# A state-space layer and two feed-forward layers on one core: the first feed-forward layer in four blocks of one piece and four of two, instead of six and three

## The chip, the cores and the metric

The kernel runs on one core of a Trainium2 chip. The metric is the device time of one execution in microseconds, smaller is better. A measurement is the median of several executions.

## What is computed

A chunked state-space scan (4 sequences, 8 heads, 768 tokens, head size 32, state size 16) gives 3072 tokens of 256 numbers. Two feed-forward layers follow, each 256 to 2048 to 256, the first with a leaky ReLU, the second with a squared ReLU:

```python
for c in range(nc):                       # chunks of 32 tokens
    cum = np.cumsum(la, axis=-1)
    M = einsum('bhin,bhjn->bhij', Cc, Bc) * L          # L: causal decay
    y[:, :, sl] = einsum('bhij,bhjd->bhid', M, xc) \
                + einsum('bhin,bhnd->bhid', Cc, state) * exp(cum)
    state = decay_full * state + sum_j(Bc x xc * decay_from_j)
x = y as (tokens, 256)
h = x @ moe_w_in;  x = maximum(0.01 * h, h) @ moe_w_out
h = maximum(x @ moe2_w_in, 0);  x = (h * h) @ moe2_w_out
```

The matrix products of the feed-forward layers are made of three TensorE products of rounded parts (high, low), so that the result keeps float32 accuracy.

## The kernel before

The tokens are cut into 12 pieces of 256 tokens (p0 to p11). The scan works piece by piece: `scan_a` and `scan_b` are generators that give way after every few instructions, and `stage(k)` runs `scan_b(k - 1)` and `scan_a(k)` side by side. What a piece gives are the tiles `yh` and `yl` (lines 448 and 449), 256 tokens wide.

One piece needs on TensorE the products S (lines 389 and 390, stationary `kbd`), Y1 (lines 418 to 420, stationary `xbh` and `xbl`) and Y2 (lines 439 and 440, stationary `sbd`). These four stationary tiles are block-diagonal, have one buffer each, and are filled by `diag` (line 353), four small DMAs on SP's queue for each tile, so 16 for a piece. SP issues in order. Ahead of the pieces p6 to p8 stand scales of their whole sequence, for which tiles `all` are loaded and squared (line 274).

The first feed-forward layer takes the pieces in blocks, `BLOCKS`: six blocks of one piece (256 columns) and three of two (512 columns). A block is one `One` object. Its hidden rows are worked in steps, 96 over all blocks: a step of a one-piece block does two groups of 128 hidden rows with 256 columns each, a step of a two-piece block one group with 512 columns. In every step `hmm` does the first product (`in_products`, lines 470 to 472), `act` evicts it (two on ScalarE, lines 507 and 508, one on VectorE, line 509), and `omm` does the second product (lines 532, 533, 538) two steps later in a block of one piece and three steps later in a block of two (`LAG`). `finish` copies the block's result (line 547). The block of p0 is in float32 (lines 493, 526). Steps are counted from 0 here: 0 to 7 are p0's block, 32 to 39 p4's, 40 to 47 p5's, and step 48 begins the block of p6 and p7.

How far the scan is emitted at a step says `due`: every block has a place (twice its first step less its `LEAD`) by which the stages for its pieces are to be emitted, with a ramp of `RATE` towards it. Weights of the second layer are prepared in between, from block `W2_FROM` on (`w_one`: lines 132, 135, 143, 152, 174, 175). This sets the order of the source. Behind it the framework's own scheduler makes each engine's final order, so that it differs from the source's by several steps.

Of the kernel before, what the change touches and what calls it, by code (L numbers as in the profile page):

```python
# [32 lines left out]
KK = 2.0**-12  # L33
E23 = float(1 << 23)

BLOCKS = [1, 1, 1, 1, 1, 1, 2, 2, 2]
NG = NP // 2
LAG = {1: 2, 2: 3}
LAG2 = 2
W_AHEAD = 4  # L40
RATE = 1.4 / KO
LEAD = [0, 4, 12, 12, 10, 8, 6, 4, 4]
W2_FROM = 3
NSTEP = 15
APART = 3
PRE = 8
# [9 lines left out]
def ssd_moe_kernel(ctx: ExitStack, tc: tile.TileContext, in1, in2, w1i, w1o, w2i, w2o, out):  # L56
# [395 lines left out]
    blocks, q0 = [], 0  # L452
    for n in BLOCKS:
        blocks.append((q0, n))
# [216 lines left out]
    for i, (p0, n) in enumerate(blocks):  # L671
        todo += [(i, list(range(m, m + 2 // n))) for m in range(0, KO, 2 // n)]
    at_ = [2 * [i for i, _ in todo].index(i) for i in range(len(blocks))]
    starts = [
        (at - lead, p0 + n + (0.5 if p0 + n <= APART else 1)) for at, lead, (p0, n) in list(zip(at_, LEAD, blocks))[1:]
    ]

    def due(at):
        return max(nb - max(RATE * (b - at), 0) for b, nb in starts)

    pend = []

# [18 lines left out]
    for i, ms in todo:  # L701
        p0, n = blocks[i]
# [6 lines left out]
        pos += 2  # L709
        ph_.act(ms)  # L710
        stages_to(due(pos + 2))
        pend.append((ph_, ms, ms[-1] == KO - 1))
        if len(pend) > LAG[n]:
# [8 lines left out]
        else:  # L722
            first_w = w_full and w_full[0][0][0] == "1"
            acc += 1.5 if first_w else 0 if i < W2_FROM else (0.4 if i < len(blocks) - 1 else 1.5)
            while acc >= 1:
# [75 lines left out]
```

## Time and profile before

| | |
|---|---|
| median of 3 runs | 606.81 us (606.45 to 608.25) |
| the profiled execution | 606.45 us, its span 604.7 us |
| TensorE busy in the span | 572.1 us (95%) |
| VectorE, ScalarE busy | 455.6 us (75%), 445.5 us (74%) |
| mean granted TensorE clock | 0.998 |

The profile prints for each engine its busy time and share of the span, and the span again in 40 slices with a digit for the busy tenths of each. A matmul is recorded longer than the distance to the next, since matmuls overlap; how fast TensorE goes is read from the starts. The timeline prints start, length, engine, line, operation and tiles, and in brackets an idle time ahead with what ended it.

### The profile page before, as it was taken

To read this page: it belongs to the slowest core of one execution; us is meant where nothing else is said; L and a number is where in the kernel's file an instruction comes from. 1 tells how busy PE (TensorE), PEld (TensorE's weight loads), DVE (VectorE), ACT (ScalarE), POOL (GpSimd) and SP (SyncE) were. 2 spreads that over 40 slices of the span, in tenths; PEclk is the share of its full clock that TensorE was granted. 3 is DMA by queue.
4 is the path that set the end of the run, shared out by engine and by line. 5 is a ranking of instruction groups with operands and counts; after the bars stand their busy time and mean duration, and the time that the engine had idled before them with its cause. 6 is when DMAs were issued, how large, how long until landed. Compare 5 with 4: busy or idle time off the path is not lost.

```text
span 604.7 us, 11654 instructions
## 1 busy us (share of the span) xinstructions
PE 572.1 (95%) x4610; PEld 516.3 (85%) x4610; DVE 455.6 (75%) x774; ACT 445.5 (74%) x715; POOL 5.2 (1%) x15
## 2 busy tenths in 40 slices
PE   0399999999999999999999999999999999999996
PEld 0388899999999878888888889989999999999996
DVE  6999989569984979567655468787777877877765
ACT  6999876479676868556665588877878777777773
POOL 3000000000000000000000000000000000000000
PEclk9999999999999999999999999999999999999999
DMA  8864845573576663131210000010000100100101
GB/s 295 289 160 129 234 111 116 129 193 92 113 187 189 163 166 36 36 62 46 69 36 0 1 2 0 2 36 1 9 28 1 35 1 2 36 1 0 36 1 35
DMA packets 113574, 46.50 MB, mean 77 GB/s; under 512 B 94448, under 2 KB 103280, under 8 KB 113520
## 3 DMA queue, kind: packets, MB, share of 16 engines
q1 hardware_dynamic: 113520, 45.76, 28.3%
q8 instruction: 36, 0.59, 0.4%
q14 instruction: 18, 0.15, 0.1%
HBM read 36.83 MB, written 3.15 MB: 66 GB/s over the span
## 4 chain that ended last, share of the span: by engine, by line
PE 86%; DVE 7%; ACT 4%; issue 2%; DMA 1%; DVEq 0%; ACTq 0%
PE hp L470 13%; PE hp L471 13%; PE hp L472 13%; PE o L532 4%; PE o L611 4%; PE o L538 4%; PE o L533 4%; PE o L609 4%; PE o L610 4%; PE oo L533 3%; PE oo L538 3%; PE oo L532 3%; PE Ym L611 3%; PE Ym L610 3%; PE Ym L609 3%
## 5 line engine op out<-in xcount | busy, mean ns | idle before, releaser
L509 DVE TENSOR_TENSOR g<-t,g 128x512 fp32r<-128x512 f32 x88 | 60.5, 687 | 52.6 <-ACT t L508 52.4
L587 DVE TENSOR_TENSOR tl<-ts,th 128x1024 fp32r<-128x1024 f32 x48 | 58.8, 1226 | 47.1 <-ACT th L585 47.1
L507 ACT ACTIVATE g<-hp 128x512 fp32r<-128x512 f32 x88 | 52.3, 594 | 47.2 <-PE o L538 33.7
L470 PE MATMUL hp<-yl,w1i 128*128 128x256 f32 (+1 forms) x256 | 83.4, 326 | 0.7 <-DVE yl L449 0.7
L471 PE MATMUL hp<-yh,w1i 128*128 128x256 f32 (+1 forms) x256 | 83.2, 325 | 0.0
L472 PE MATMUL hp<-yh,w1i 128*128 128x256 f32 (+1 forms) x256 | 83.0, 324 | 0.0
L575 ACT ACTIVATE b<-hp 128x512 f32<-128x512 f32 x96 | 57.2, 596 | 33.0 <-PE hp L472 32.8
L470 PE MATMUL hp<-xl,w2i 128*128 128x512 f32 x192 | 75.4, 393 | 0.0
L471 PE MATMUL hp<-xh,w2i 128*128 128x512 f32 x192 | 75.3, 392 | 0.0
L472 PE MATMUL hp<-xh,w2i 128*128 128x512 f32 x192 | 74.8, 389 | 0.0
L585 ACT CAST th<-ts 128x1024 fp32r<-128x1024 f32 x48 | 50.3, 1047 | 16.8 <-DVE ts L584 16.8
L470 PEld LDWEIGHTS hp<-yl,w1i 128*128 128x128 f32 x256 | 48.7, 190 | 4.9 <-DVE yl L449 1.1
L508 ACT ACTIVATE t<-hp 128x512 f32<-128x512 f32 x88 | 52.2, 593 | 0.0
L472 PEld LDWEIGHTS hp<-yh,w1i 128*128 128x128 f32 x256 | 48.7, 190 | 3.7
L471 PEld LDWEIGHTS hp<-yh,w1i 128*128 128x128 f32 x256 | 48.7, 190 | 3.7
L576 ACT ACTIVATE b<-b 128x1024 f32<-128x1024 f32 x48 | 50.9, 1061 | 1.1
L586 DVE TENSOR_TENSOR bl<-b,bh 128x768 fp32r<-128x768 f32 x48 | 45.7, 952 | 0.0
L582 DVE TENSOR_TENSOR ts<-b 128x512 f32<-128x512 f32 x48 | 33.2, 691 | 14.5 <-ACT b L576 13.5
L472 PEld LDWEIGHTS hp<-xh,w2i 128*128 128x128 f32 x192 | 36.1, 188 | 7.8
L470 PEld LDWEIGHTS hp<-xl,w2i 128*128 128x128 f32 x192 | 36.2, 189 | 6.3
L471 PEld LDWEIGHTS hp<-xh,w2i 128*128 128x128 f32 x192 | 36.2, 189 | 5.8
L581 ACT CAST bh<-b 128x768 fp32r<-128x768 f32 x48 | 40.1, 835 | 1.3
(167 smaller groups left out, 1571.4 us busy)
## 6 DMA issues: line engine op xcount, KB each, us to landing
in<-in SPq DMA_DIRECT2D x12, 640.0 KB, 4.9
in<-in SPq DMA_DIRECT2D x12, 512.0 KB, 5.7
all<-in SPq DMA_DIRECT2D x15, 384.0 KB, 4.3
wst<-w1i SPq DMA_DIRECT2D x8, 512.0 KB, 6.6
wst<-w1o SPq DMA_DIRECT2D x8, 512.0 KB, 6.4
wst<-w2i SPq DMA_DIRECT2D x8, 512.0 KB, 7.4
wst<-w2o SPq DMA_DIRECT2D x8, 512.0 KB, 4.2
out_t<-r SPq DMA_DIRECT2D x24, 128.0 KB, 1.7
```

The lines of the kernel that those rows point to most:

```text
L470: nc.tensor.matmul(hp, wh[:, k, c], xl[:, :, k], start=(k == 0), stop=False)
L471: nc.tensor.matmul(hp, wh[:, k, c], xh[:, :, k], start=False, stop=False)
L472: nc.tensor.matmul(hp, wl[:, k, c], xh[:, :, k], start=False, stop=(k == KI - 1))
L507: nc.scalar.activation(g[:, 0], hp, AF.Lrelu)
L508: nc.scalar.activation(t, hp, AF.Lrelu)
L509: nc.vector.tensor_tensor(g[:, 1], t, g[:, 0].bitcast(F32), ALU.subtract)
L532: nc.tensor.matmul(self.o[d], wl[:, c], gh, start=(m == 0 and (d == 0 or self.n == 2)), stop=False, **kw)
L575: nc.scalar.activation(b[:, 2 * i : 2 * i + 2], hp.rearrange("p (n t) -> p n t", n=2), AF.Relu)
L576: nc.scalar.activation(b, b, AF.Square)
L585: nc.scalar.copy(th, t)
L586: nc.vector.tensor_tensor(bl, b[:, 1:], bh.bitcast(F32), ALU.subtract)
L587: nc.vector.tensor_tensor(tl, t, th.bitcast(F32), ALU.subtract)
```

## The change

The pieces p4 and p5 form one block of two pieces. The table `LEAD` has new numbers from the fifth entry on, the scan's ramp towards the new block is 1.3 times as steep, and second-layer weights start in the same block as the two-piece work. The number of steps stays 96.

```diff
-BLOCKS = [1, 1, 1, 1, 1, 1, 2, 2, 2]
+BLOCKS = [1, 1, 1, 1, 2, 2, 2, 2]
-LEAD = [0, 4, 12, 12, 10, 8, 6, 4, 4]
-W2_FROM = 3
+LEAD = [0, 4, 12, 12, 11, 12, 8, 6]
+W2_FROM = 4
...
     starts = [
-        (at - lead, p0 + n + (0.5 if p0 + n <= APART else 1)) for at, lead, (p0, n) in list(zip(at_, LEAD, blocks))[1:]
+        (at - lead, p0 + n + (0.5 if p0 + n <= APART else 1), RATE * (1.3 if i == 4 else 1))
+        for i, (at, lead, (p0, n)) in enumerate(zip(at_, LEAD, blocks))
+        if i > 0
     ]
...
-        return max(nb - max(RATE * (b - at), 0) for b, nb in starts)
+        return max(nb - max(r * (b - at), 0) for b, nb, r in starts)
```

The engines' orders are the same in both kernels up to step 31 of the first layer (TensorE), up to the scale factors of p6's sequence (VectorE, ScalarE), and on SP up to the loads for p7. Then they part. On SP, before; `kbd`, `xbh` and `xbl` are here those of p6, `sbd<-t_2262` is that of p5, and the `kbd` behind it that of p7:

```order
L123 DMA wst<-w2i 128x2x256 x2
L353 DMA kbd<-kmx 32x16x32 x4
L353 DMA xbh<-xh 32x16x32 x4
L353 DMA xbl<-xl 32x16x32 x4
L353 DMA sbd<-t_2262 32x16x32 x4
L353 DMA kbd<-kmx 32x16x32 x4
```

And on SP in the changed kernel, with `sbd<-t_2042` that of p5:

```order
L315 DMA all<-in 128x3x256 x2
L353 DMA xbh<-xh 32x16x32
L353 DMA kbd<-kmx 32x16x32 x4
L353 DMA xbh<-xh 32x16x32 x3
L353 DMA xbl<-xl 32x16x32 x4
L353 DMA sbd<-t_2042 32x16x32 x4
L353 DMA kbd<-kmx 32x16x32 x4
```

Two weight loads ahead of it became two loads for scales; p5's `sbd` still stands behind the twelve transfers of p6.

On TensorE, before, behind the last `omm` rows that step 31 issues: the `hmm` of step 32 begins, which reads p4 alone, and S of p6 is put into it.

```order
L538 MATMUL oo<-g,w1o 128x256 x4
L470 MATMUL hp<-yl,w1i 128x256
L471 MATMUL hp<-yh,w1i 128x256
L472 MATMUL hp<-yh,w1i 128x256
...
L470 MATMUL hp<-yl,w1i 128x256
L389 LDWEIGHTS kbd
L389 MATMUL S<-ch,kbd 128x32
```

On TensorE in the changed kernel, from the last `omm` of p3's block to the first `hmm` of the block of p4 and p5; the first L389 is S of p7, the L418 is Y1 of p6, and the L439 is Y2 of p5:

```order
L538 MATMUL oo<-g,w1o 128x256 x4
L439 LDWEIGHTS sbd
L439 MATMUL Y<-qh,sbd 128x32
...
L389 LDWEIGHTS kbd
L389 MATMUL S<-ch,kbd 128x32
...
L418 LDWEIGHTS xbh
L418 MATMUL Y<-mkh,xbh 128x48
...
L470 MATMUL hp<-yl,w1i 128x512
L471 MATMUL hp<-yh,w1i 128x512
L472 MATMUL hp<-yh,w1i 128x512
```

Y2 of p5 stood in step 35 and Y1 of p6 and S of p7 in step 36; now all three stand ahead of step 32, which reads p4 and p5 together. S of p7 is split: eight of its 16 column groups stand ahead of Y1 of p6 and eight behind.

## Rows read from the trace of the kernel before

**Rows 1.** The page: engine busy time and share, and TensorE in 40 slices.

```profile
PE 572.1 (95%) x4610; PEld 516.3 (85%) x4610; DVE 455.6 (75%) x774; ACT 445.5 (74%) x715; POOL 5.2 (1%) x15
...
PE   0399999999999999999999999999999999999996
```

**Rows 2.** Timeline of TensorE, two stretches without other work; first column start.

```profile
107.54 0.28 PE L470 MATMUL hp<-yl,w1i 128*128 128x256 f32 x1
...
108.50 0.28 PE L472 MATMUL hp<-yh,w1i 128*128 128x256 f32 x1
...
299.72 0.39 PE L470 MATMUL hp<-yl,w1i 128*128 128x512 f32 x1
...
301.99 0.39 PE L471 MATMUL hp<-yh,w1i 128*128 128x512 f32 x1
```

**Rows 3.** Groups by line and shape: count, busy us, mean ns.

```profile
L470 PE MATMUL hp<-yl,w1i 128*128 128x256 f32 x160 | 46.0, 287 | 0.7 <-DVE yl L449 0.7
L470 PE MATMUL hp<-yl,w1i 128*128 128x512 f32 x96 | 37.5, 390 | 0.0
```

**Rows 4.** Timeline of TensorE where the first two-piece block begins its second product.

```profile
210.49 0.40 PE L533 MATMUL o<-g,w1o 128*128 128x512 f32 x1
212.19 0.47 PE L532 MATMUL o<-g,w1o 128*128 128x512 f32 x1 [1.30 <-DVE yf L547]
```

**Rows 5.** Timeline of TensorE, steps 32 to 40: S of p6, Y2 of p5, Y1, S.

```profile
145.12 0.28 PE L470 MATMUL hp<-yl,w1i 128*128 128x256 f32 x1
...
145.97 0.19 PE L389 MATMUL S<-ch,kbd 128*128 128x32 f16 x1
...
146.78 0.36 PE L471 MATMUL hp<-yh,w1i 128*128 128x256 f32 x1
...
155.62 0.19 PE L439 MATMUL Y<-qh,sbd 128*128 128x32 f16 x1
...
156.43 0.36 PE L472 MATMUL hp<-yh,w1i 128*128 128x256 f32 x1
...
158.91 0.20 PE L418 MATMUL Y<-mkh,xbh 128*128 128x48 f16 x1
...
160.20 0.18 PE L389 MATMUL S<-ch,kbd 128*128 128x32 f16 x1
...
161.00 0.37 PE L471 MATMUL hp<-yh,w1i 128*128 128x256 f32 x1
...
173.00 0.28 PE L470 MATMUL hp<-yl,w1i 128*128 128x256 f32 x1
```

**Rows 6.** Timeline of SP's queue in the same stretch; second column: time that issuing took.

```profile
141.38 2.67 SPq L353 DMA_DIRECT2D kbd<-kmx  x4
144.16 2.60 SPq L353 DMA_DIRECT2D xbh<-xh  x4
146.87 3.75 SPq L353 DMA_DIRECT2D xbl<-xl  x4
150.71 2.60 SPq L353 DMA_DIRECT2D sbd<-t  x4
153.42 2.61 SPq L353 DMA_DIRECT2D kbd<-kmx  x4
```

**Rows 7.** DMA issues from 140 to 160 us: count, size, median us from issue to landing.

```profile
kbd<-kmx SPq DMA_DIRECT2D x8, 32.0 KB, 2.1
sbd<-t SPq DMA_DIRECT2D x4, 32.0 KB, 2.0
```

**Rows 8.** Timelines of ScalarE and VectorE: what p6's transfers and p5's result wait for.

```profile
139.91 0.71 ACT L375 ACTIVATE xh<-in,sc 128x512 f16<-128x512 f32 x1
...
140.57 0.74 DVE L372 SCALAR_TENSOR_TENSOR kmx<-in,sc,him 128x512 f16<-128x512 f32 x1
...
144.70 0.71 DVE L431 STREAM_TRANSPOSE t<-shl 128x512 f16<-128x512 f16 x1
...
158.02 0.74 DVE L449 SCALAR_TENSOR_TENSOR yl<-Y,fac,yh 128x512 fp32r<-128x512 f32 x1
```

**Rows 9.** Windows: length, then PE, PEld, DVE, ACT, POOL busy with counts, granted clock, DMA share, GB/s.

```profile
107.54:113.30 5.76, 5.76 (x50) 5.76 (x49) 2.05 (x4) 2.63 (x5) 0.00 (x0) 1.00 0.46 53
599.00:604.70 5.70, 0.79 (x7) 0.58 (x5) 2.32 (x4) 0.00 (x0) 0.00 (x0) 0.74 0.27 92
```

**Rows 10.** Windows of line 493 alone: length, PE and PEld busy with counts, clock, DMA share, GB/s.

```profile
29.50:34.80 5.30, 5.28 (x12) 4.22 (x13) 1.00 0.79 245
34.80:36.30 1.50, 1.50 (x8) 1.32 (x7) 1.00 0.38 44
```

**Rows 11.** Timelines of SP and TensorE: p7's `sbd`, and its Y2 in step 46.

```profile
186.04 2.61 SPq L353 DMA_DIRECT2D sbd<-t  x4
...
192.81 0.19 PE L439 MATMUL Y<-qh,sbd 128*128 128x32 f16 x1
```

## Prediction

> **What bounds the kernel now.** I read the busy shares first, then the slices, then TensorE's starts. TensorE is busy 95% of the span, and from the third slice to the last but one every slice has a 9 [rows 1]. So a change gains only what it takes out of TensorE's own stream, and costs every microsecond for which it makes TensorE wait. The next question is what a matmul costs in that stream. In a stretch with no other work, eight matmuls of 256 columns go from 107.54 to 108.50 us, 0.120 us each, and ten of 512 columns from 299.72 to 301.99, 0.227 us each [rows 2]. These starts are the price; the busy means of 287 and 390 ns [rows 3] hold the overlap and are not.
>
> The third question is when the result of each piece is there and when TensorE first needs it. p5's `yl` begins at 158.02 and takes 0.74 us [rows 8], so p5 is there at 158.8. TensorE needs it at 173.00, at the first product of its block; p4's block begins at 145.12 [rows 5]. The margin of p5 is 14.2 us, and the eight steps of p4 are what fills it.
>
> **The change part by part.**
>
> *Fewer, longer matmuls.* A group of 128 hidden rows takes 12 matmuls (six in `hmm`, six in `omm`), a block 16 groups, so 192; the counts agree (160 is five blocks by 32, 96 is three by 32) [rows 3]. Two blocks of 256 columns become one of 512: 384 x 0.120 = 46.1 us become 192 x 0.227 = 43.6 us. TensorE saves 2.5 us. The 192 weight loads saved lie under other matmuls and count nothing by themselves. Evictions stay: both kinds of step evict one tile of 512 columns.
>
> The Trainium skill, "TensorE: Matmul & The Clock Gate", section "Back-to-back issue gap", gives columns / 2.4 + 2.5 ns for a warm matmul: 109.2 and 215.8 ns. By that the saving would be 0.5 us instead of 2.5. The starts above contradict it (120 and 227 ns), and the sum goes by the starts.
>
> *The first two-piece block's gap.* Where the one-piece blocks end, the second product of the next block must wait for the copy of the last result; 1.70 us lie between two starts where 0.23 would do [rows 4], so 1.5 us are lost. In the change this border lies between p3's block and the new one. There TensorE stands still for another reason (next), and the copy, queued on VectorE ahead of p5's `yl`, is done within that time. I take 1.5 us as saved; bounds 0 and 1.5.
>
> *The new wait.* Step 32 now reads p4 and p5 together, so p5 loses its margin: it is needed where p4's block began, at 145.12. Is it earlier than before? The source emits its stages some steps earlier, but up to TensorE's step 31 and SP's loads for p7 the engines' orders are the same, and the rest of p5's chain hangs on SP. In both kernels p5's `sbd` stands on SP behind twelve transfers of p6. These wait for p6's `xh` and `kmx` (done at 140.6 and 141.3 [rows 8]), and those for scales that stand in the part that is the same. p5's transpose, which `sbd` copies, ends at 145.4 [rows 8] and then waits until 150.71 for the queue [rows 6]. The sixteen transfers take from 141.38 to 153.31 [rows 6].
>
> In the change the queue begins with one `xbh`. ScalarE does one copy more ahead of `xh` and two weight steps less, which gives `xh` at about 141.1, so I let the same twelve microseconds run from 141.1 and the last `sbd` begin at 152.4. It lands 2.0 us after its issue [rows 7], at 154.4; allowing 0.3 us for the semaphore, Y2 of p5 begins at 154.7 and takes 0.81 us (155.62 to 156.43 [rows 5]), to 155.5. From the end of Y2 to the end of `yl` went 2.3 us before (156.43 to 158.76), so p5 is there at 157.8.
>
> But TensorE has two more things ahead of step 32: S of p7 and Y1 of p6. p7's `kbd` is the next on SP, 2.7 us behind `sbd` [rows 6]: its last transfer begins at 155.1 and lands 2.1 us later [rows 7], at 157.2. Half of S (0.40), Y1 (1.29) and the other half (0.40) [rows 5] end at 159.3. This is later than p5's 157.8, so step 32 begins at 159.3.
>
> What does TensorE do from 145.12 to there? Its own work is two `omm` of 12 x 0.120, S of p6 (0.81), Y2 of p5 (0.81), Y1 of p6 (1.29) and S of p7 (0.80): 6.6 us, done at 151.7 if nothing waited. The wait is 159.3 - 151.7 = 7.6 us. Bounds: with no slow issue (the 3.75 us of `xbl` at 2.6) and 0.3 less for the semaphore 6.1 us; with one slow issue more and landings late by 2 us 10.5 us. What is queued behind it is all of block 4; VectorE and ScalarE have p6's and p7's scan meanwhile.
>
> *The clock.* About 5 us of the wait are one stretch, before Y2 of p5. The execution's first products of line 493 follow such waits: 12 starts in 5.30 us, then 8 in 1.50 [rows 10]; the first ran at half speed, whatever the clock column prints there (1.00). In starts 0.44 us became 0.21 (seven whole distances in 1.50), so the 12 cost 2.7 us more. At the end the granted clock falls too, to a mean of 0.74 over the last window, in which TensorE is done after 0.79 us [rows 9]. I charge the new wait once, 2.7 us; bounds 0 and 3.2 (the short scan products at half speed, 0.5).
>
> The Trainium skill, the same page, Part 1, says that half speed is the default state of TensorE and that a spell without activity puts it back there until work has run for some time. No row before shows a wait of 5 us in the middle, so the sentence decides only how likely this term is.
>
> *What is moved at no cost.* Weight preparation for the second layer starts eight steps later, and the last of its tiles is finished in that layer instead. VectorE and ScalarE are busy 75% and 74% [rows 1], so there is room; without it a tile would cost about 1 us.
>
> *Sum*, against the profiled execution's 606.45 us (span 604.7; the median of the three runs is 0.36 higher): 606.45 - 2.5 - 1.5 + 7.6 + 2.7 = 612.75 us. I say 612.8.
>
> **The rivals.**
>
> *No wait* (the other side). If p5, S of p7 and Y1 of p6 were done by 151.7, only the savings are left: 606.45 - 2.5 - 1.5 = 602.5. For it: there is room on VectorE earlier (2.05 of 5.76 us busy from 107.54 on [rows 9]), and the table asks for the stages earlier. Against it: the orders up to step 31 are the same, so that room is not used, and 16 transfers from about 141 on do not end by 148. The break-even lies at a wait of 4 us without a slower clock, 1.3 us with it.
>
> *The wait without the clock's fall.* Y2, S and Y1 stand within the wait, and TensorE would stay at full speed: 610.0.
>
> *Later waits as well.* From step 32 on each scan product stands one to three steps earlier than before. p7's `sbd` was issued until 188.65, landed at about 190.6 and was used at 192.81 [rows 11], 2.2 us of slack; in the change its Y2 stands in step 43 instead of 46. With step 32 at 159.3, the first three steps of 6 x 0.227, eight more of 12 x 0.227, 2.9 us of scan and 2.7 for the clock, TensorE is there at about 190.7, just level. A slip of 1 to 4 us gives 614 to 617.
>
> **How the numbers follow.** Forecast (wait and clock, 612.8): 0.60. Wait without the clock: 0.18. Later waits as well: 0.12. No wait or a short one: 0.10, of which 0.07 faster by over 0.3% (604.6 and less) and 0.03 about level. 0.3% (1.8 us) is what a measurement here can tell from no change. That gives faster 0.07, same 0.04, slower 0.89. The range: the low end is the least wait with no clock loss, 606.45 - 4.0 + 6.1 = 608.6; the high end is the long wait with the clock, 606.45 - 4.0 + 10.5 + 3.2 = 616.2, and a little for later waits, 617.
>
> **What would show it.** In the profile after: p5's `yl` ends between 156 and 160 us; the last `omm` of p3's block is followed by an idle stretch of TensorE of about 5 us with p5's `sbd` at its end; the first product of 512 columns begins at 158 to 162 us. The products behind it start 0.43 us apart for some microseconds, or the granted clock of that window is below 1. In the block of p4 and p5 the starts are then 0.227 us apart. No idle time of 1.5 us stands at the border to p6. I am wrong if the first 512-column product begins before 153 us, or if TensorE waits elsewhere for more than 3 us.

## The result, and the profile after

The change makes the kernel slower: 612.85 us (median of four, 612.29 to 613.23) against 606.63 us (median of four), a ratio of 1.010 with a 95% interval of 1.0075 to 1.0126. Measured again on another chip beside the experiments (e8) the ratio is 1.0106 (1.0091 to 1.0122). The profiled execution shown here took 613.23 us, its span is 611.4 us: 6.7 us more than the span before.

The page of the changed kernel, engine busy time, then TensorE and its granted clock in 40 slices, to be read beside [rows 1]:

```profile
PE 572.6 (94%) x4418; PEld 506.8 (83%) x4418; DVE 456.4 (75%) x773; ACT 444.2 (73%) x714; POOL 5.2 (1%) x15
...
PE   0399999997799999999999999999999999999996
...
PEclk9999999999799999999999999999999999999999
```

There are 192 matmuls less (4418 for 4610). Two slices, the 10th and 11th, are no longer full, and in the 11th the clock is down too. So most of the loss must be looked for between 137 and 168 us. The timeline of TensorE there; brackets give idle time and what ended it:

```profile
147.65 0.18 PE L389 MATMUL S<-ch,kbd 128*128 128x32 f16 x1 [1.12 <-DMA kbd<-kmx]
...
154.65 0.19 PE L439 MATMUL Y<-qh,sbd 128*128 128x32 f16 x1 [3.93 <-DMA sbd<-t]
...
157.57 0.18 PE L389 MATMUL S<-ch,kbd 128*128 128x32 f16 x1 [1.93 <-DMA kbd<-kmx]
...
160.35 0.77 PE L470 MATMUL hp<-yl,w1i 128*128 128x512 f32 x1
160.92 0.63 PE L471 MATMUL hp<-yh,w1i 128*128 128x512 f32 x1
161.35 0.63 PE L472 MATMUL hp<-yh,w1i 128*128 128x512 f32 x1
161.78 0.55 PE L470 MATMUL hp<-yl,w1i 128*128 128x512 f32 x1
162.16 0.39 PE L471 MATMUL hp<-yh,w1i 128*128 128x512 f32 x1
162.38 0.39 PE L472 MATMUL hp<-yh,w1i 128*128 128x512 f32 x1
```

These are S of p6, Y2 of p5, S of p7 and the first product of the block of p4 and p5, which is step 32. Before, step 32 began at 145.12 [rows 5], here at 160.35. Every one of the three waits ends with a transfer of SP's queue, whose timeline answers [rows 6]:

```profile
141.44 0.61 SPq L353 DMA_DIRECT2D xbh<-xh  x1
142.15 2.60 SPq L353 DMA_DIRECT2D kbd<-kmx  x4
144.79 1.98 SPq L353 DMA_DIRECT2D xbh<-xh  x3
146.88 3.62 SPq L353 DMA_DIRECT2D xbl<-xl  x4
150.60 2.60 SPq L353 DMA_DIRECT2D sbd<-t  x4
153.31 2.60 SPq L353 DMA_DIRECT2D kbd<-kmx  x4
```

p5's `sbd` is issued at 150.60, where it was at 150.71 before. The rows on VectorE that answer the last two of [rows 8] are p5's transpose `t`, which `sbd` copies, and p5's `yl`:

```profile
144.13 0.71 DVE L431 STREAM_TRANSPOSE t<-shl 128x512 f16<-128x512 f16 x1
...
157.08 0.74 DVE L449 SCALAR_TENSOR_TENSOR yl<-Y,fac,yh 128x512 fp32r<-128x512 f32 x1
```

`t` is done at 144.84 and stands for 5.8 us until the queue takes it. `yl` ends at 157.8, one microsecond earlier than before, while the first product that reads it, at 173.00 before, now stands ahead of everything else of its block. The clock is read from windows (length, then PE, PEld, DVE, ACT, POOL busy with counts, clock, DMA share, GB/s):

```profile
150.60:155.20 4.60, 0.67 (x24) 0.55 (x23) 2.06 (x3) 0.87 (x2) 0.00 (x0) 1.00 0.37 43
155.30:162.00 6.70, 4.77 (x97) 4.40 (x94) 5.36 (x7) 2.94 (x5) 0.00 (x0) 0.50 0.81 235
```

0.50 is the lower of the two levels, 1.2 GHz. The clock is still full in the longest of the waits, and falls when Y2 of p5 is almost done. At the border between the new block and that of p6 and p7, where p6's block began with a gap [rows 4], 0.44 us lie between the starts:

```profile
217.58 0.40 PE L533 MATMUL o<-g,w1o 128*128 128x512 f32 x1
218.02 0.50 PE L532 MATMUL o<-g,w1o 128*128 128x512 f32 x1
```

And in the second layer there is a wait that the kernel before does not have, at the first `o` product of its second group:

```profile
403.59 0.35 PE L609 MATMUL o<-bh,wl 128*128 128x256 f32 x1 [0.40 <-DVE r L625]
```

Start to start, it costs 0.56 us more than an undisturbed pair (402.81 to 403.59, less 0.22).

### The profile page after: what moved, and what is told of

It is laid out like the page before. It is cut to its first block, busy times and chain, and to the rows that moved or that the text cites. A ratio compares the mean times of both kernels' runs of the same rounds, so it can differ in the third digit from the quotient of the medians.

```text
span 611.4 us, 11244 instructions
## 1 busy us (share of the span) xinstructions
PE 572.6 (94%) x4418; PEld 506.8 (83%) x4418; DVE 456.4 (75%) x773; ACT 444.2 (73%) x714; POOL 5.2 (1%) x15
## 4 chain that ended last, share of the span: by engine, by line
PE 85%; DVE 7%; ACT 3%; SPq 2%; issue 2%; DMA 1%; DVEq 0%; ACTq 0%
PE hp L470 13%; PE hp L471 13%; PE hp L472 13%; PE o L532 5%; PE o L533 5%; PE o L538 5%; PE o L611 4%; PE o L609 4%; PE o L610 4%; PE Ym L611 3%; PE Ym L610 3%; PE Ym L609 3%; SPq L353 2%; PE hp L493 2%; PE oo L533 1%
## 5 line engine op out<-in xcount | busy, mean ns | idle before, releaser
L470 PE MATMUL hp<-yl,w1i 128*128 128x512 f32 (+1 forms) x224 | 78.3, 350 | 0.7 <-DVE yl L449 0.7
L471 PE MATMUL hp<-yh,w1i 128*128 128x512 f32 (+1 forms) x224 | 77.7, 347 | 0.0
L472 PE MATMUL hp<-yh,w1i 128*128 128x512 f32 (+1 forms) x224 | 77.4, 345 | 0.0
L532 PE MATMUL o<-g,w1o 128*128 128x512 f32 x128 | 50.9, 398 | 0.1
L533 PE MATMUL o<-g,w1o 128*128 128x512 f32 x128 | 50.1, 391 | 0.0
L470 PEld LDWEIGHTS hp<-yl,w1i 128*128 128x128 f32 x224 | 42.6, 190 | 6.2 <-DVE yl L449 1.1
L471 PEld LDWEIGHTS hp<-yh,w1i 128*128 128x128 f32 x224 | 42.7, 191 | 5.0
L472 PEld LDWEIGHTS hp<-yh,w1i 128*128 128x128 f32 x224 | 42.6, 190 | 5.1
L472 PEld LDWEIGHTS hp<-xh,w2i 128*128 128x128 f32 x192 | 36.1, 188 | 7.8
```

What stands on the lines that cost most here:

```text
L470: nc.tensor.matmul(hp, wh[:, k, c], xl[:, :, k], start=(k == 0), stop=False)
L471: nc.tensor.matmul(hp, wh[:, k, c], xh[:, :, k], start=False, stop=False)
L472: nc.tensor.matmul(hp, wl[:, k, c], xh[:, :, k], start=False, stop=(k == KI - 1))
L532: nc.tensor.matmul(self.o[d], wl[:, c], gh, start=(m == 0 and (d == 0 or self.n == 2)), stop=False, **kw)
L533: nc.tensor.matmul(self.o[d], wh[:, c], gh, start=False, stop=False, **kw)
```

## The experiments

All ratios are to the kernel before, run on the same chip.

**e1: p5's `sbd` ahead of p6's transfers.** The changed kernel, with one stage emitted in another order:

```diff
-        if k <= APART:
+        if k <= APART or k == 6:
             yield from b
```

and stage 6 counted with twice as many substeps, as the stages that run so already are.

> The changed kernel, but in stage 6 the second half of p5's scan is emitted before the first half of p6's, as the stages up to 3 already are. On SP p5's sbd then stands behind two transfers of p6 instead of twelve, and on TensorE Y1 of p6 and S of p7 stand in steps 33 and 36, behind the first product of the new block. Theory (the new wait is p5's chain through SP's queue, plus the two scan products of p6 and p7 ahead of step 32): p5's yl ends at about 151 instead of 157.8, the wait shrinks from 7.5 us to 0 to 2 us, the clock does not fall, and the time is about 604 us (602.5 to 606). Rival (the wait is set by p5's own chain on VectorE and ScalarE, whatever SP does): p5's yl still ends after 156, and the time stays at 611 to 613.

It took 607.81 us, a ratio of 1.0038 (1.0021 to 1.0055). VectorE, SP, TensorE, and a window of the clock:

```profile
142.78 0.71 DVE L431 STREAM_TRANSPOSE t<-shl 128x512 f16<-128x512 f16 x1
...
143.56 3.23 SPq L353 DMA_DIRECT2D sbd<-t  x4
...
148.32 0.18 PE L439 MATMUL Y<-qh,sbd 128*128 128x32 f16 x1 [0.82 <-DMA sbd<-t]
149.63 0.18 PE L389 MATMUL S<-ch,kbd 128*128 128x32 f16 x1 [0.36 <-PE Y L440]
151.61 0.50 PE L470 MATMUL hp<-yl,w1i 128*128 128x512 f32 x1 [1.03 <-DVE yl L449]
...
152.90:156.00 3.10, 3.10 (x9) 2.12 (x9) 3.10 (x4) 1.81 (x4) 0.00 (x0) 0.50 0.46 52
```

p5's `sbd` is issued 7 us earlier, p5's `yl` ends at 151.6, as expected, and the new block begins at 151.61 instead of 160.35. The edit moves p5's work forward on every engine, but its transpose ends only 1.3 us earlier (143.49 for 144.84). So it was the queue's order that set p5's time; the rival falls. The time was missed by almost 4 us, and the clock, expected to hold, fell: three short waits remain, 2.7 us start to start, the matmuls behind them start 0.43 us apart again for about 3 us, and the wait in the second layer is there too.

**e2: the emission alone.** The kernel before with the change's `LEAD`, ramp and `W2_FROM`, its blocks kept. The table has an entry more here, and 27 puts p5's place where the merged block has it (2 x 40 - 27 = 2 x 32 - 11):

```diff
-LEAD = [0, 4, 12, 12, 10, 8, 6, 4, 4]
+LEAD = [0, 4, 12, 12, 10, 27, 12, 8, 6]
-W2_FROM = 3
+W2_FROM = 4
...
+        (at - lead, p0 + n + (0.5 if p0 + n <= APART else 1), RATE * (1.3 if i == 5 else 1))
```

> The kernel before with its blocks (six of one piece, three of two), but with the change's emission: the same places, ramp and start of second-layer weights. Theory (the emission by itself costs nothing, only a block that needs p4 and p5 together turns p5's time into a wait): p5's yl ends at 157 to 159 as before, TensorE does not wait for it, and the time is 606.6 us within 1.5. Rival (the earlier emission crowds VectorE, ScalarE and SP, and that is what costs): 609 us or more, with waits of TensorE between steps 29 and 48.

607.18 us, a ratio of 1.0025 (1.0014 to 1.0036), so 1.5 us slower than the kernel before on this chip. p5's `yl` ends at 159.0 and TensorE does not wait for it, as the theory said. But the emission is not free, where the theory had put it at nothing: S of p6 waits, since one `xbh` now stands ahead of its `kbd` on SP and the last of the four lands 3.2 us after its issue, where 2.0 is usual, and the wait in the second layer appears here as well (0.55 us start to start).

```profile
147.08 0.18 PE L389 MATMUL S<-ch,kbd 128*128 128x32 f16 x1 [0.93 <-DMA kbd<-kmx]
```

**e3: the blocks alone**, that is the kernel before with the new blocks and its own table cut to fit; ramp and `W2_FROM` are the old ones:

```diff
-BLOCKS = [1, 1, 1, 1, 1, 1, 2, 2, 2]
+BLOCKS = [1, 1, 1, 1, 2, 2, 2, 2]
...
-LEAD = [0, 4, 12, 12, 10, 8, 6, 4, 4]
+LEAD = [0, 4, 12, 12, 10, 6, 4, 4]
```

> The new blocks, four of one piece and four of two, but with the old table (12, 12, 10, then 6, 4, 4), the old ramp for every block and second-layer weights from the fourth block on. The old ramp reaches further ahead, so the scan stands earlier against the steps from step 2 on: Y2 of p5 in step 30 instead of 31, and TensorE's early steps stand behind scan products. Theory (until p5 is there the scan is the slower chain, and where the wait stands is a matter of order): the wait in front of the new block is smaller than 7.5 us, but steps 2 to 31 take longer by about what it saves or more; the time is 609 to 614 us. Rival (the steeper ramp and later places are what costs): under 606 us.

620.82 us, a ratio of 1.0248 (1.0232 to 1.0264), worse than either guess. TensorE's waits from 55 to 80 us (us in total, times, longest), then the window of the slow clock:

```profile
PE Y L418 <- ACT mkh L405: 4.9, 1, 4.9
PE Y L439 <- DMA sbd<-t: 3.8, 1, 3.8
PE hp L493 <- DVE raw L148: 3.1, 1, 3.1
...
58.20:75.30 17.10, 7.14 (x117) 6.14 (x118) 13.29 (x19) 8.87 (x16) 0.00 (x0) 0.50 0.89 248
```

With these places the old ramp starts earlier for a piece that is due with its neighbour, and the scan products it puts ahead of the first block's own work are waited for there. The theory's first half held (no wait stands directly in front of the new block, which begins at 160.92, and p5's `yl` ends at 159.1), its size did not: with one more of 0.8 us the early waits add up to 12.6 us, and TensorE runs at half its clock for 17 us. A wait of 2.35 us at 225.09, where the new block ends, is followed by half the clock once more:

```profile
225.09 0.50 PE L532 MATMUL o<-g,w1o 128*128 128x512 f32 x1 [2.35 <-ACT yf L547]
...
225.50:228.80 3.30, 3.30 (x9) 2.38 (x8) 3.30 (x7) 3.30 (x7) 0.00 (x0) 0.50 0.43 52
```

So the change's ramp and places together spare the early steps; this run does not tell the one from the other.

**e4: work put into the wait.** The changed kernel and 20 products into a tile that nobody reads, in the last step of p3's block:

```diff
+        if i == 3 and m == KO - 2:
+            idle = ph.tile([P, 512], F32, tag="h", name="idle")
+            wh, _ = w_of("1i", m)
+            for _ in range(20):
+                nc.tensor.matmul(idle, wh[:, 0, 0:P], ys[1][0][:, :, 0], start=True, stop=True)
```

> The changed kernel with 20 products of 512 columns more, in the last step of p3's block, into a PSUM tile that nobody reads: 4.5 us of TensorE work put into the wait in front of p5's Y2. Theory (the wait costs twice, once itself and once by the half clock behind it, 1.6 us in the changed kernel's trace): p5's Y2 and the new block begin where they do without them or up to 0.7 us earlier, the products behind start 0.227 us apart, the granted clock stays at 1, and the time falls by 1 to 2 us to about 611.3. Rival (the work is on the path): the time rises by up to 4.5 us to 617.

613.22 us, a ratio of 1.0123 (1.0106 to 1.014); the change alone has 1.0106 (1.0091 to 1.0122, e8, on another chip). The two intervals overlap, so the 4.5 us of work cost nothing that can be measured, and gained nothing. TensorE, then a window:

```profile
147.41 3.90 PE L722 MATMUL idle<-yh,w1i 128*128 128x512 f32 x16
...
157.60 0.20 PE L418 MATMUL Y<-mkh,xbh 128*128 128x48 f16 x1 [2.33 <-DVE yl L449]
...
154.00:160.50 6.50, 4.04 (x113) 3.69 (x112) 4.64 (x7) 2.43 (x5) 0.00 (x0) 0.76 0.70 201
```

It was free room, so the rival falls. But the clock fell all the same, later, near the end of what is left of the wait (155.1 to 157.6), and the scan products behind it ran slowly: the test of the clock's price failed, and this run does not settle it. It showed something that the prediction had passed over: Y1 of p6 waits for p5's `yl`, since both use the one buffer of Y. So p5's chain itself ends with Y1 of p6, not with `yl`.

**e5: the state first in the stages 4 to 6.** As e1, with p4 and p5 brought forward as well, in this line and in the count of substeps:

```diff
-        if k <= APART:
+        if k <= 6:
             yield from b
```

> As e1_state_first, but for the stages 4, 5 and 6: the second half of one piece's scan is emitted before the first half of the next. p4's and p5's sbd stand on SP ahead of the next piece's transfers, Y1 of p5 stands in step 26 instead of 29. Theory (what is left in e1 of the wait, 2.7 us and the half clock behind it, is p5 still being 3 to 6 us late, so an earlier p5 takes both away): p5's yl ends before 149, TensorE waits less than 1 us in front of the new block, the clock stays at 1, and the merged block's saving comes out: 1 to 3 us below the kernel before, a ratio of 0.995 to 0.999. Rival (the saving of merging is used up by other things in the changed order, as the 1.4 us that e2 lost with no merged block): a ratio of 1.000 to 1.004.

605.00 us, a ratio of 0.9984 (0.9975 to 0.9993): faster than both kernels, by 1 us (0.4 to 1.5) than the one before, by 7 us than the change. SP, VectorE and TensorE:

```profile
136.27 2.62 SPq L353 DMA_DIRECT2D sbd<-t  x4
...
144.44 0.75 DVE L449 SCALAR_TENSOR_TENSOR yl<-Y,fac,yh 128x512 fp32r<-128x512 f32 x1
...
146.08 0.47 PE L470 MATMUL hp<-yl,w1i 128*128 128x512 f32 x1
146.39 0.39 PE L471 MATMUL hp<-yh,w1i 128*128 128x512 f32 x1
```

p5 is there at 145.2, 12.6 us earlier than in the change (its transpose, too, ends 8.6 us earlier, at 136.2), the block begins at 146.08 with no idle time ahead, and its matmuls start 0.23 us apart from the second on. Run again beside e9 (e10) it has 604.98 us and 0.9986 (0.9977 to 0.9995).

> e5 unaltered, beside e9 on the same chip. A ratio of 0.996 to 1.000 to the kernel before; no wait in front of the block of p4 and p5, and the clock at 1 to the end of the work.

**e6: the same order without the merged block**, that is the kernel before with the edit of e5.

> The kernel before, its blocks and tables kept, with the emission of e5 in the stages 4 to 6. It tells what of e5's time is the order of the scan and what the merged block. Theory: p5 has a margin of 14 us here, so an earlier p5 gains nothing: 1.000 within 0.003 of the kernel before, and e5 is below it by the saving of merging (2.5 us) and up to 1.5 us of the gap at the border. Rival (the order of the scan is worth something by itself): 0.997 or less.

608.95 us, a ratio of 1.0053 (1.004 to 1.0065). Neither guess was right: the order by itself costs 3 us. TensorE's waits from 75 to 215 us:

```profile
PE o L532 <- DVE yf L547: 1.3, 1, 1.3
PE Y L439 <- DMA sbd<-t: 0.7, 1, 0.7
PE Y L419 <- DVE mkl L410: 0.6, 2, 0.4
PE S L389 <- DMA kbd<-kmx: 0.4, 1, 0.4
```

The first is the old gap at the border. The kernel before has that one and 0.4 of the third. So scan products that stand earlier on TensorE now wait a little each. Together they are 1.3 us more; what the rest of the 3 us is, these rows don't say. Against e5, which has the same order of the scan, the whole change (blocks, table, ramp and later weights) is worth 1.0053 - 0.9984 = 0.0069, or 4.2 us, give or take one. This is not the two forecast savings alone: the waits of 0.7 and 0.4 us for `sbd` and `kbd` are not in e5, and e5 keeps two short ones for `yf` (0.26 and 0.17 us, at 158.61 and 208.53) where e6 has 1.3.

**e7: p6 and p7 apart too**, eight blocks of one piece:

```diff
-BLOCKS = [1, 1, 1, 1, 1, 1, 2, 2, 2]
-LEAD = [0, 4, 12, 12, 10, 8, 6, 4, 4]
+BLOCKS = [1, 1, 1, 1, 1, 1, 1, 1, 2, 2]
+LEAD = [0, 4, 12, 12, 10, 8, 8, 6, 4, 4]
```

> The kernel before with p6 and p7 apart as well: eight blocks of one piece and two of two. No block needs a piece earlier, so only the price of short matmuls is left, with the other sign. Theory (0.120 us for 256 columns and 0.227 for 512): 384 x 0.120 - 192 x 0.227 = 2.5 us slower, a ratio of 1.004, with the gap of 1.5 us at the border between p7 and p8 instead of p5 and p6. Rival (columns alone count, and a fixed cost of about 2.5 ns a matmul): 0.5 us, a ratio of 1.001.

607.70 us, a ratio of 1.0026 (1.0016 to 1.0036), 1.6 us slower (1.0 to 2.2). The gap at the border did not stay: 0.54 us between these starts,

```profile
262.10 0.40 PE L533 MATMUL o<-g,w1o 128*128 128x512 f32 x1
262.64 0.47 PE L532 MATMUL o<-g,w1o 128*128 128x512 f32 x1
```

where it was 1.70 [rows 4], so 1.2 us came back, which the expectation had not foreseen. 2.5 - 1.2 = 1.3 us lies in the interval. The rival's 0.5 us, less the same 1.2, would have been a gain.

**e9: weights of the second layer in time.** e5, with the preparation's share raised so that as much is done before the second layer as in the kernel before:

```diff
-            acc += 1.5 if first_w else 0 if i < W2_FROM else (0.4 if i < len(blocks) - 1 else 1.5)
+            acc += 1.5 if first_w else 0 if i < W2_FROM else (0.47 if i < len(blocks) - 1 else 1.5)
```

> e5 with 0.47 instead of 0.4 steps of second-layer weight preparation for each step of the blocks from the fourth on, so that as many are done before the second layer as in the kernel before (48 steps by 0.47 instead of 56 by 0.4). Theory (the weight tiles that the later start pushes into the second layer cost a wait of 0.55 us before the second group's first o product, near 394 us in e5, and that is all they cost): this wait is gone and the time is 0.4 to 0.8 us below e5. Rival (the preparation now crowds the scan in the blocks before): the wait is gone but the time is that of e5 or more.

605.09 us, a ratio of 0.9988 (0.9979 to 0.9997), level with e5. The wait in the second layer is gone, so it did come from the later start; the time did not follow, as the rival had it. In the profiled execution the short waits of TensorE for the copies `yf` (line 547, near 160 and 210 us) are 0.9 us in all, where e5 has 0.5, and one of 0.5 us for `sbd` near 108 us stands before the edit can act. What else holds the time, these rows don't say.

**e8: the change unaltered**, beside e5 to e7.

> The changed kernel unaltered, on the same chip as the three runs beside it, so that they and the runs of before compare without a change of chip. Both theories: a ratio of 1.010 to 1.013, the wait of 7.5 us in three pieces in front of the block of p4 and p5, the half clock behind it.

612.38 us, a ratio of 1.0106. The wait in front of Y2 of p5 is there again, half a microsecond longer, and the clock stays down for longer:

```profile
153.43 0.21 PE L439 MATMUL Y<-qh,sbd 128*128 128x32 f16 x1 [4.42 <-DMA sbd<-t]
...
152.10:162.30 10.20, 6.99 (x120) 6.24 (x121) 6.69 (x10) 4.14 (x8) 0.00 (x0) 0.50 0.75 196
```

## Why the prediction was right

The time (612.85 for 612.8) and the mechanism came out. That the time agrees to 0.1 us is luck: the clock's term was too large by 1.1 us, and 1.4 us came in that the sum did not have. Step by step:

- **Fewer, longer matmuls, -2.5 us.** Holds. Counts and starts are as in [rows 2, 3], and e7, which does it the other way, has +1.6 us where 2.5 less the gap's 1.2 give 1.3. The formula of the Trainium skill ("TensorE: Matmul & The Clock Gate", section "Back-to-back issue gap"), which that section gives for an isolated matmul and by which it would be 0.5 us, does not agree with e7 nor with the starts.
- **The gap at the border, -1.5 us.** 0.2 us of it are left at the next border (217.58), so 1.3 us. That p3's copy would be done within the wait was right. The 4.2 us between e5 and e6 are near the 4.0 of these two terms, but they hold other waits too (e6), so they do not prove the sum.
- **The new wait, 7.6 us.** Start to start less what the matmuls need, the three waits are 1.28, 4.09 and 2.09: 7.5 us. p5's `yl` was forecast to end at 157.8 and ends at 157.8; Y2 of p5 was put at 154.7 and begins at 154.65. The 0.3 us allowed there for the semaphore have no row; from the start of the last `sbd` issue to Y2 went 2.1 us (152.57 to 154.65) where 2.3 were allowed. The stretch before Y2 was 4.1 us and not about 5, since S of p6 had waited 1.3 us already. That p5 does not come earlier was the decisive step, and e1 shows its reason: with `sbd` ahead of most of p6's transfers, p5 comes 6 us earlier, though its transpose ends only 1.3 us earlier. Step 32 was put at 159.3 and begins at 160.35; 0.7 us of that is the clock's fall, which slows S and Y1 ahead of it. What the prediction left out is that Y1 of p6 also waits for `yl` (e4); here S of p7 came just as late, so it cost nothing.
- **The clock, 2.7 us.** The term that was mis-sized. Four matmuls of 512 columns take 1.81 us instead of 0.91 (160.35 to 162.16), and S of p7 with Y1 of p6 2.78 instead of 2.09 (157.57 to 160.35): 1.6 us. The stretch in [rows 10], from which the 2.7 was taken, holds 12 long products; here the clock is down for nearly 7 us, but 2.1 us of them are idle, where it costs nothing, and 2.8 us hold short scan products, so that only four long ones are left. (That the 12 ran at half speed, whatever the clock column prints there, is borne out by e3: six of line 493, from 70.44 to 73.24, start 0.47 us apart on average where the column prints 0.50.) In e8 seven of the long matmuls ran slowly (159.12 to 162.25, 3.1 us for 1.6), so the term moves by about half a microsecond between executions. That the clock fell because TensorE waited fits every run: it falls behind the waits in e1, e3, e4 and e8, and stays at 1 in e2 and e5, which have only single waits of under a microsecond. It is argued from this, not shown; a run that takes the fall alone away was not found.
- **What is moved at no cost.** Wrong: the weights that slid into the second layer cost a wait of 0.56 us there, though VectorE and ScalarE have a quarter of their time free. e9 takes it away, but does not get faster by it.
- **The sum.** -2.5 - 1.3 + 7.5 + 1.6 + 0.6 = 5.9; the spans differ by 6.7. About 0.4 us is there before the change can act (step 29 begins at 134.93 for 134.53); the rest is spread over short waits that no single row carries.

Of the rivals, the wait without the clock's fall would have been 610.0 and is out by the windows at 0.50. Later waits did not come: Y2 of p7 began at 192.5 without a wait longer than 0.2 us. The side on which the kernel is faster exists, and e5 is it, but by another order than the change's table gave.

## What to carry to other kernels

Two units of work that are merged are due together, at the time of the earlier one: look up in the trace when the later half is ready and what stands ahead of it in every in-order queue, a DMA queue above all, before counting the saving. A table that asks for work earlier in the source moves nothing where the engines' final orders stay the same up to that point; compare the orders, not the table. Here merging took nearly 4 us out of TensorE's stream, and that became a gain, of 1 us, only when the later half's chain and its transfers were put ahead of work that nobody waited for yet.

## What the runs showed of the hardware

- A matmul of 256 columns cost 0.120 us in the stream and one of 512 columns 0.227 us: two short ones cost 13 ns more than the long one that replaces them, where I would have expected next to nothing.
- SP took 0.65 us to issue each small block-diagonal transfer, and now and then over 1.5 us (the four of `xbl` of p6 took 3.62 us, and 3.75 in the kernel before). They landed 2.0 us after the issue as a rule, and the last `kbd` of p6 in the change 3.4 us after it. A piece's sixteen transfers are 11 to 12 us of an in-order queue that counts as neither busy nor bound in the page's first part.
- Behind a wait of 3.9 us in the middle of the work TensorE's granted clock went from 1.00 to 0.50, and so it did behind one of 2.35 us (e3, at 225.09), in one of 2.33 us (e4), and behind three of 0.8, 0.4 and 1.0 us in a row (e1). A single wait of 1.30 us (the kernel before, at 212.19), or of 0.9 and less (e2, e5), left it at 1.00. What of the waits decides it, these runs don't show.
